# A chained attention and two-MoE kernel: the second MoE's weights converted two thirds of the program earlier, by way of DRAM

## The chip, the cores and the metric

The kernel runs on one core of one Trainium2 chip. The metric is the device time of one execution, in microseconds (us); the median of three runs is 1712.07 us, the runs lie between 1711.86 and 1712.95. Engines are named as the profile names them: PE is TensorE's matmul, PEld its weight load, DVE is VectorE, ACT is ScalarE, POOL is GpSimd, SP is SyncE, which issues all of this kernel's DMAs.

## The reference, cut to what matters

A linear attention, an MoE (a two-layer perceptron with s * relu(h)^2 + b between the layers) and a second MoE (with h * sigmoid(1.702 h)), one behind the other, all in float32:

```python
kv = einsum('bhsd,bhse->bhde', k, v)                 # 8 batches, 8 heads, 576 x 64
o  = einsum('bhsd,bhde->bhse', q, kv)
x  = o / sqrt(mean(o * o) + 1e-6) * g_norm           # -> 4608 tokens x 512
x  = (s * relu(x @ w_in)**2 + b) @ w_out             # 512 -> 2048 -> 512
h  = x @ w2_in
x  = (h * sigmoid(1.702 * h)) @ w2_out
```

The weights reach the device as 64-bit words, two 32-bit halves for each value, and are turned into float32 there.

## The kernel before

**Tiles and steps.** The 4608 tokens are cut into NB = 9 blocks of 512. A block of an MoE has NF = 16 steps, one for each 128 of the 2048 inner features. So there are 2 x 9 x 16 = 288 steps, numbered i = 0 to 287: steps 0 to 143 are the first MoE (block j has steps 16j to 16j + 15), steps 144 to 287 the second. Every matmul operand is split into a high and a low part (hi and lo), and three products are summed: h takes 12 matmuls of 128x512 (`mlp_h`, L255), o takes 12 (`mlp_o`, L295). In the first MoE o's second matmul is the first that reads gl.

**The order within a step** is written out by hand at the end of the kernel and kept as it stands (`manual_schedule`): `mlp_h` of this step on PE; side work of slot 2i; `mlp_act` of this step (relu L263 and square L264 on ACT; in the second MoE sigmoid on ACT, product on DVE); `mlp_o` of the step before on PE; `mlp_g` of this step (gh on ACT, L275 or L278; r, L276, and gl, L279, on DVE); at a block's first step the results of the block before are copied out (`mlp_store`: two by ACT, L304, two by DVE, L302, then four DMAs on SP, L306 or L308); side work of slot 2i + 1. So PE runs h(i), o(i-1), h(i+1), o(i), and ACT and DVE have from the end of h(i) to the second matmul of o(i) for relu to gl. Each engine works through its queue in the order of the program: on ACT, what stands in slot 2i comes before the step's relu.

**Side work** is a list of (slot, order of entry, function). Entries with the same slot keep the order in which they were entered: attention before the second MoE's inputs, these before its weights. There are four kinds.

- The k and v products (`kv_load`, `kv_product`), up to slot 49. Their inputs lie in two buffers of the pool `kp` with the tag "kv", of 5 KB a partition each.
- Attention of block j, during block j - 1, for each head pair p = 0 to 3: `att_product` (PE; ACT's square and sh, L190; DVE's sl, L191) at slot 32(j-1) + 7 + 6p, `att_mean` (PE's two matmuls, then three operations on ACT, L201 to L203) two slots later, `att_newton` (three operations on DVE, L208 to L210) two later, `att_split` (xh on ACT, L219, and the subtraction xl on POOL, L222) two later, which is the slot of the next pair's `att_product`. These slots are odd: each is the second half of a step. `q_load` stands five slots before `att_product`.
- The second MoE's inputs: `x2_load` (SP, from the DRAM tile x2d) and `x2_split` (ACT, L239, and POOL, L240), four for each block.
- The weights. A unit is one of 16 pieces of w_in or w_out (`which` 0 or 1, `f` 0 to 15): 512 KB raw, 128 x 1024 words. `weight(load, slot, gap, conv_at, ...)` enters `w_load` (one DMA on SP, L82 or L87) at `load`, and at slot + gap * conv_at the four parts `w_low` (two operations on ACT, L94 and L95), `w_words` (four on DVE, L101 to L104), `w_hi` (one on ACT, L111) and `w_lo` (one on DVE, L116).

**The second MoE's weights before.** Their 32 units go into the buffers of the first MoE's weights (pool `wp`, one buffer for each unit), so each raw unit waits until the first MoE has used that piece for the last time, in its last block (j = 8, steps 128 to 143). Unit n has slot 259 + 1.75 n with the parts at +0, +1, +2.5 and +4.5, and its load three slots earlier: slots 256 to 318, steps 128 to 159.

The program below prints the functions that the diff touches and what calls them.

Of the kernel before, what the change touches and what calls it, by code (L numbers as in the profile page):

```python
# [7 lines left out]
F32 = mybir.dt.float32  # L8
F32R = mybir.dt.float32r
U32 = mybir.dt.uint32  # L10
# [3 lines left out]
P = 128  # L14
# [4 lines left out]
NF = DFF // P  # L19
NB = B * S // T  # L20
# [4 lines left out]


START = [(-61, -60, -54, -52, -45), (-59, -54, -53, -47, -42), (-54, -48, -48, -43, -41), (-50, -49, -46, -40, -36)]
CONV = [(0, 1, 2, 3), (-0.5, 0, 1, 1.5), (0, 1, 2.5, 4.5)]


@with_exitstack
def kernel(ctx: ExitStack, tc: tile.TileContext, qT, kv_h, kvt, cst,
# [6 lines left out]
    nc = tc.nc  # L39
# [3 lines left out]
    wp = ctx.enter_context(tc.tile_pool(name="wp", bufs=1))  # L43
# [4 lines left out]
    kp = ctx.enter_context(tc.tile_pool(name="kp", bufs=2))  # L48
    dp = ctx.enter_context(tc.tile_pool(name="dp", bufs=1, space=bass.MemoryType.DRAM))
# [26 lines left out]
    conv, W = {}, {}  # L76

    def w_load(m, f, which):
        raw = wp.tile([P, 512, 2], U32, tag=f"w{which}_{f}", name="raw")
        src = w_raw[m][which]  # L80
        if which == 0:
            nc.sync.dma_start(  # L82
                out=raw.rearrange("p (k c) t -> p k (c t)", k=NP),
                in_=src.rearrange("(k p) c -> p k c", p=P)[:, :, f * 2 * P:(f + 1) * 2 * P],
            )
        else:
            nc.sync.dma_start(out=raw.rearrange("p c t -> p (c t)"), in_=src[f * P:(f + 1) * P, :])  # L87
        conv[m, f, which] = raw
# [17 lines left out]

    def w_hi(m, f, which):
        a = conv[m, f, which]
        w = wp.tile([P, 2, 512], F32R, tag=f"w{which}_{f}", name=f"w{which}_{f}")
        W[m, f, which] = (w[:, 0, :], w[:, 1, :])  # L110
        act.activation(w[:, 0, :], a.bitcast(F32), AF.Copy)  # L111

    def w_lo(m, f, which):
        a = conv.pop((m, f, which))
        hi, lo = W[m, f, which]
        dve.tensor_sub(out=lo, in0=a.bitcast(F32), in1=hi.bitcast(F32))  # L116


    kvin, kvs, qin, xT, done = {}, {}, {}, {}, set()
# [196 lines left out]
    def at(slot, fn, *a):  # L316
        side.append((slot, len(side), fn, a))

    def weight(load, slot, gap, conv_at, *unit):
        at(load, w_load, *unit)  # L320
        for n, (i, fn) in enumerate(zip(conv_at, (w_low, w_words, w_hi, w_lo))):
            at(slot + gap * i, fn, *unit)
# [7 lines left out]
    def attention(slots, j, p, o_at, ms_at):  # L330
        at(slots[0], att_product, j, p, o_at)
        at(slots[1], att_mean, j, p, ms_at)
        at(slots[2], att_newton, j, p)
        at(slots[3], att_split, j, p)
# [4 lines left out]
    for p in range(NP):  # L339
        kv_work(-99 + p, START[p][0], 0, p, (pa, pb)[p % 2])  # L340
        at(-99 + p, q_load, 0, p)
        attention(START[p][1:], 0, p, (ps_o, f"o{p}"), (ps_h, "h"))
    weight(-128, -58.5, 3.5, CONV[0], 0, 0, 0)
    weight(-89, -48.5, 4, CONV[0], 0, 1, 0)


    units = [(f - w, w) for f in range(1, NF + 1) for w in range(2) if f - w < NF][1:]
    for n, (f, w) in enumerate(units):
        weight(n - 5, n - 1, 1, CONV[1], 0, f, w)

# [5 lines left out]
    for j in range(1, NB):  # L356
        for p in range(NP):
            slot = 2 * NF * (j - 1) + 7 + 6 * p
# [6 lines left out]
    for j in range(NB):  # L365
        for p in range(NP):
            slot = 2 * NF * (NB + j - 1) + 1 + 3.5 * p
            at(slot, x2_load, j, p)
            at(slot + 3, x2_split, j, p)
    for n in range(2 * NF):  # L370
        slot = 2 * NF * (NB - 1) + 3 + 1.75 * n
        weight(slot - 3, slot, 1, CONV[2], 1, n // 2, n % 2)

    side.sort(key=lambda e: e[:2])
    side.reverse()
# [60 lines left out]
```

## Time and profile before

| | before |
|---|---|
| median of three runs | 1712.07 us |
| the profiled execution's own time | 1712.43 us |
| its span, first to last instruction | 1710.6 us |
| mean granted clock of TensorE | 0.996 |
| PE busy | 1685.7 us (99%) |
| PEld busy | 1380.0 us (81%) |
| ACT busy | 745.7 us (44%) |
| DVE busy | 721.9 us (42%) |
| POOL busy | 96.1 us (6%) |
| DMA: read from, written to HBM | 72.22 MB, 19.79 MB |

A busy share is a mean over stages that differ, and matmuls are pipelined, so that a PE which is shown as busy can still run slower than it might. A step's length is read from the timeline instead: from the first matmul of an h or o to that of the next one. Step numbers are had by counting the h groups of twelve (the trace does not name steps). In a timeline a row is: start in us from the span's beginning, length in us, engine, line, operation, tiles written and read, shape, count, and in brackets the engine's idle time before it and what ended that. In a table by windows a row is: stretch, its length, then the busy time of PE, PEld, DVE, ACT and POOL with the count of instructions, the granted clock, the DMA engines' busy share and GB/s.

### The profile page before, as it was taken

Reading aid. Unit: us, or ns where it says so; the run is one execution under the profiler, and the core shown is the slowest. Engines: PE = TensorE matmul, PEld = TensorE weight load, DVE = VectorE, ACT = ScalarE, POOL = GpSimd, SP = SyncE. Lnnn points to the kernel's source line nnn. Section 1 sums busy time; section 2 is a strip of 40 time slices with the busy share of each in tenths; the row PEclk is TensorE's granted clock in tenths of the full one; section 3 lists DMA queues with packets and bytes.
Section 4 is the critical chain, followed back from the end, with each engine's and each line's share of the span. In section 5 each row is a group of like instructions: output and inputs, shape, how many; then the busy total and the mean of one; then the engine's idle time right before and its main releaser. Section 6 shows DMA issues by size and latency. Waiting matters only on the chain.

```text
span 1710.6 us, 18774 instructions
## 1 busy us (share of the span) xinstructions
PE 1685.7 (99%) x7460; PEld 1380.0 (81%) x7460; DVE 721.9 (42%) x1110; ACT 745.7 (44%) x1218; POOL 96.1 (6%) x82
## 2 busy tenths in 40 slices
PE   7999999999999999999999999999999999999998
PEld 5877888888888888888877788888888888888887
DVE  5997233433434343434578842222222222222222
ACT  5776455545455454555676532222222222222222
POOL 1000000000000000000000000000000000101000
PEclk8999999999999999999999999999999999999999
DMA  7863401010100001010434110101010101000000
GB/s 239 272 210 104 121 19 46 7 47 7 40 13 32 22 1 53 1 44 7 160 124 164 46 50 1 49 0 48 2 44 7 44 7 38 12 27 24 20 7 25
DMA packets 67655, 93.22 MB, mean 54 GB/s; under 512 B 13808, under 2 KB 40432, under 8 KB 67568
## 3 DMA queue, kind: packets, MB, share of 16 engines
q1 hardware_dynamic: 67568, 92.04, 17.0%
q8 instruction: 58, 0.95, 0.2%
q14 instruction: 29, 0.24, 0.0%
HBM read 72.22 MB, written 19.79 MB: 54 GB/s over the span
## 4 chain that ended last, share of the span: by engine, by line
PE 89%; DVE 7%; DMA 1%; ACT 1%; issue 1%; SPq 0%; DVEq 0%; ACTq 0%
PE o L295 42%; PE h L255 42%; PE o_ps L182 2%; DVE cu L103 1%; PE kv L149 1%; DVE w L116 1%; PE ms L198 1%; DVE ca L104 1%; DVE cu L102 1%; DVE gl L279 1%; DVE cu L101 1%; PE kv L150 1%; DVE r L276 0%; DMA kv_in<-in_kv 0%; DVE r L267 0%
## 5 line engine op out<-in xcount | busy, mean ns | idle before, releaser
L255 PE MATMUL h<-xh,w 128*128 128x512 f32 x2304 | 769.0, 395 | 0.1
L255 PEld LDWEIGHTS h<-xh,w 128*128 128x128 f32 x2304 | 433.2, 188 | 95.0 <-issue 1.7
L255 PE MATMUL h<-xl,w 128*128 128x512 f32 x1152 | 449.0, 390 | 0.0
L295 PE MATMUL o<-gh,w 128*128 128x512 f32 x1152 | 378.2, 389 | 0.0
L295 PE MATMUL o<-w,gh 128*128 128x512 f32 x1152 | 356.2, 390 | 3.4 <-ACT gh L278 3.3
L279 DVE TENSOR_TENSOR gl<-r,gh 128x512 fp32r<-128x512 f32 x288 | 228.9, 795 | 113.6 <-ACT gh L278 100.6
L267 DVE TENSOR_TENSOR r<-h,r 128x512 f32<-128x512 f32 x144 | 99.5, 691 | 414.8 <-ACT r L266 414.8
L266 ACT ACTIVATE r<-h 128x512 f32<-128x512 f32 x144 | 85.8, 596 | 414.8 <-PE h L255 414.7
L295 PEld LDWEIGHTS o<-w,gh 128*128 128x128 f32 x1152 | 216.7, 188 | 49.7 <-ACT gh L278 5.0
L255 PEld LDWEIGHTS h<-xl,w 128*128 128x128 f32 x1152 | 216.8, 188 | 47.7 <-issue 2.7
L295 PEld LDWEIGHTS o<-gh,w 128*128 128x128 f32 x1152 | 216.2, 188 | 45.2 <-ACT gh L275 0.4
L276 DVE TENSOR_SCALAR r<-r,cst_sb 128x512 f32<-128x512 f32 x144 | 78.7, 547 | 379.3 <-ACT gh L275 379.1
L295 PE MATMUL o<-gl,w 128*128 128x512 f32 x576 | 224.9, 390 | 3.7 <-DVE gl L279 3.7
L295 PE MATMUL o<-w,gl 128*128 128x512 f32 x576 | 225.0, 391 | 0.0
L263 ACT ACTIVATE r<-h 128x512 f32<-128x512 f32 x144 | 85.7, 595 | 249.3 <-PE h L255 249.3
L278 ACT ACTIVATE gh<-r 128x512 fp32r<-128x512 f32 x144 | 91.1, 633 | 124.7 <-DVE r L267 124.7
L295 PEld LDWEIGHTS o<-gl,w 128*128 128x128 f32 x576 | 108.1, 188 | 28.8 <-DVE gl L279 6.5
L295 PEld LDWEIGHTS o<-w,gl 128*128 128x128 f32 x576 | 108.3, 188 | 24.1 <-DVE gl L279 1.7
L275 ACT ACTIVATE gh<-r,cst_sb 128x512 fp32r<-128x512 f32 x144 | 117.5, 816 | 4.8
L264 ACT ACTIVATE r<-r 128x512 f32<-128x512 f32 x144 | 91.0, 632 | 4.6
L222 POOL TENSOR_TENSOR xl<-y,xh 128x512 fp32r<-128x512 f32 x36 | 47.6, 1323 | 773.7 <-ACT xh L219 414.0
L240 POOL TENSOR_TENSOR xl<-x,xh 128x512 fp32r<-128x512 f32 x36 | 46.8, 1301 | 698.3 <-ACT xh L239 568.4
(53 smaller groups left out, 846.1 us busy)
## 6 DMA issues: line engine op xcount, KB each, us to landing
raw<-in_w_in SPq DMA_DIRECT2D x32, 512.0 KB, 5.7
kv_in<-in_kv SPq DMA_DIRECT2D x32, 512.0 KB, 4.6
raw<-in_w_out SPq DMA_DIRECT2D x32, 512.0 KB, 6.3
x2d<-st SPq DMA_DIRECT2D x36, 256.0 KB, 2.1
x<-x2d SPq DMA_DIRECT2D x36, 256.0 KB, 2.9
out<-st SPq DMA_DIRECT2D x36, 256.0 KB, 2.1
kv_in<-in_kvt SPq DMA_DIRECT2D x32, 64.0 KB, 4.3
qq<-in_qT SPq DMA_DIRECT2D x8, 256.0 KB, 5.1
```

Of the source, the lines that this page charges most:

```text
L222: pool.tensor_sub(out=xl[:, p, :], in0=x, in1=xh[:, p, :].bitcast(F32))
L240: pool.tensor_sub(out=xl[:, p, :], in0=t, in1=xh[:, p, :].bitcast(F32))
L255: pe.matmul(h, lhsT=a[:, cc], rhs=x[:, c, :], start=(n == 0), stop=(n == 3 * NP - 1))
L263: act.activation(r, h, AF.Relu)
L264: act.activation(r, r, AF.Square)
L266: act.activation(r, h, AF.Sigmoid, scale=1.702)
L267: dve.tensor_mul(out=r, in0=h, in1=r)
L275: act.activation(gh, r, AF.Identity, scale=s_col, bias=b_col)
L276: dve.tensor_scalar(out=r, in0=r, scalar1=s_col, scalar2=b_col, op0=ALU.mult, op1=ALU.add)
L278: act.activation(gh, r, AF.Copy)
L279: dve.tensor_sub(out=gl, in0=r, in1=gh.bitcast(F32))
L295: pe.matmul(o, lhsT=a, rhs=x, start=(f == 0 and n == 0), stop=(f == NF - 1 and n == 2))
```

## The change

The 32 units of the second MoE are loaded and converted during the first MoE, in the two "kv" buffers that the k and v products no longer need. Raw words go into one ("raw2"), hi and lo into the other ("w2"). Unit n has slot 60 + 6n (60 to 246), the parts at +0, +1, +2.5 and +4, and its load two slots earlier: a unit every three steps, steps 30 to 125. At +5.5 a new function `w2_store` writes hi and lo (512 KB) to a DRAM tile. During the first MoE's last block a new function `w2_load` reads them into the buffers of the first MoE's weights, each piece after that block has used it: slot 258 + n + n % 2, steps 129 to 145. All new DMAs are on SP. 16.8 MB more are written to DRAM and 16.8 MB more are read.

```diff
-CONV = [(0, 1, 2, 3), (-0.5, 0, 1, 1.5), (0, 1, 2.5, 4.5)]
+CONV = [(0, 1, 2, 3), (-0.5, 0, 1, 1.5), (0, 1, 2.5, 4)]
...
     def w_load(m, f, which):
-        raw = wp.tile([P, 512, 2], U32, tag=f"w{which}_{f}", name="raw")
+        if m == 0:
+            raw = wp.tile([P, 512, 2], U32, tag=f"w{which}_{f}", name="raw")
+        else:
+            raw = kp.tile([P, 512, 2], U32, tag="kv", name="raw2")
...
     def w_hi(m, f, which):
         a = conv[m, f, which]
-        w = wp.tile([P, 2, 512], F32R, tag=f"w{which}_{f}", name=f"w{which}_{f}")
+        if m == 0:
+            w = wp.tile([P, 2, 512], F32R, tag=f"w{which}_{f}", name=f"w{which}_{f}")
+        else:
+            w = kp.tile([P, 2, 512], F32R, tag="kv", name="w2")
+            w2[f, which] = w
...
+    w2, w2d = {}, [[dp.tile([P, 2, 512], F32, name=f"w2d{which}_{f}") for which in range(2)] for f in range(NF)]
+
+    def w2_store(f, which):
+        nc.sync.dma_start(out=w2d[f][which], in_=w2.pop((f, which)).bitcast(F32))
+        del W[1, f, which]
+
+    def w2_load(f, which):
+        w = wp.tile([P, 2, 512], F32R, tag=f"w{which}_{f}", name=f"w{which}_{f}")
+        nc.sync.dma_start(out=w.bitcast(F32), in_=w2d[f][which])
+        W[1, f, which] = (w[:, 0, :], w[:, 1, :])
...
     for n in range(2 * NF):
-        slot = 2 * NF * (NB - 1) + 3 + 1.75 * n
-        weight(slot - 3, slot, 1, CONV[2], 1, n // 2, n % 2)
+        slot = 60 + 6 * n
+        weight(slot - 2, slot, 1, CONV[2], 1, n // 2, n % 2)
+        at(slot + 5.5, w2_store, n // 2, n % 2)
+        at(2 * NF * (NB - 1) + 2 + n + n % 2, w2_load, n // 2, n % 2)
```

## Rows read from the trace of the kernel before

**Rows 1.** Windows: a plain block, the conversion stretch, and its longest gap.
```profile
461.00:548.00 87.00, 87.00 (x386) 71.81 (x385) 33.78 (x46) 45.45 (x70) 5.12 (x4) 1.00 0.06 18
...
896.00:991.00 95.00, 90.73 (x386) 72.29 (x385) 78.34 (x129) 55.60 (x96) 5.66 (x4) 0.98 0.27 94
944.00:951.00 7.00, 4.24 (x13) 3.04 (x12) 6.10 (x12) 3.21 (x6) 0.00 (x0) 0.76 0.29 105
```

**Rows 2.** Timeline of PE: the first matmuls of steps 128 and 160.
```profile
822.16 0.39 PE L255 MATMUL h<-xh,w 128*128 128x512 f32 x1
...
1007.04 0.39 PE L255 MATMUL h<-xh,w 128*128 128x512 f32 x1
```

**Rows 3.** Timelines of PE, DVE and ACT, steps 141 and 142.
```profile
898.42 0.39 PE L295 MATMUL o<-gh,w 128*128 128x512 f32 x1
...
903.86 0.40 PE L295 MATMUL o<-gh,w 128*128 128x512 f32 x1
905.15 0.50 PE L295 MATMUL o<-gl,w 128*128 128x512 f32 x1 [0.89 <-DVE gl L279]
...
898.65 0.42 DVE L101 TENSOR_SCALAR cu<-cu 128x512 f32<-128x512 f32 x1
...
904.40 0.69 DVE L279 TENSOR_TENSOR gl<-r,gh 128x512 fp32r<-128x512 f32 x1
...
901.01 0.63 ACT L111 ACTIVATE w<-ca 128x512 fp32r<-128x512 f32 x1 [3.15 <-DVE ca L104]
901.55 0.58 ACT L263 ACTIVATE r<-h 128x512 f32<-128x512 f32 x1
...
903.55 0.65 ACT L94 ACTIVATE ca<-raw 128x512 uint32<-128x512 uint32 x1
...
904.66 0.62 ACT L111 ACTIVATE w<-ca 128x512 fp32r<-128x512 f32 x1
```

**Rows 4.** Timelines of ACT, DVE, POOL and PE, an attention cycle (steps 69, 70).
```profile
481.97 0.63 ACT L203 ACTIVATE y<-y 128x512 f32<-128x512 f32 x1
483.30 0.60 ACT L263 ACTIVATE r<-h 128x512 f32<-128x512 f32 x1 [0.70 <-PE h L255]
...
488.74 0.60 ACT L263 ACTIVATE r<-h 128x512 f32<-128x512 f32 x1 [3.33 <-PE h L255]
...
495.10 0.60 ACT L263 ACTIVATE r<-h 128x512 f32<-128x512 f32 x1 [1.45 <-PE h L255]
...
486.10 0.69 DVE L279 TENSOR_TENSOR gl<-r,gh 128x512 fp32r<-128x512 f32 x1
...
488.16 0.75 DVE L210 SCALAR_TENSOR_TENSOR y<-o_ps,g_col,y 128x512 f32<-128x512 f32 x1
...
491.54 1.79 DVE L279 TENSOR_TENSOR gl<-r,gh 128x512 fp32r<-128x512 f32 x1
493.75 0.69 DVE L191 TENSOR_TENSOR sl<-sq,sh 128x512 fp32r<-128x512 f32 x1 [0.41 <-ACT sh L190]
...
491.51 1.28 POOL L222 TENSOR_TENSOR xl<-y,xh 128x512 fp32r<-128x512 f32 x1 [38.21 <-issue]
...
495.12 0.39 PE L295 MATMUL o<-gl,w 128*128 128x512 f32 x1
```

**Rows 5.** Timelines of DVE and SP, the first step of a block (step 64).
```profile
457.53 0.69 DVE L279 TENSOR_TENSOR gl<-r,gh 128x512 fp32r<-128x512 f32 x1
...
459.48 0.69 DVE L302 COPY st<-o 128x512 f32<-128x512 f32 x1 [0.65 <-DMA x2d<-st]
...
457.36 3.16 SPq L306 DMA_DIRECT2D x2d<-st  x4
```

**Rows 6.** The tile raw, 820 to 900 us: its loads, 512 KB each.
```profile
DMA to landing us min/median/max: 3.5/4.3/5.4
```

**Rows 7.** Timeline of PE, the longest gap after the start (step 149).
```profile
947.38 1.22 PE L295 MATMUL o<-w,gh 128*128 128x512 f32 x2 [2.77 <-ACT gh L278]
```

**Rows 8.** The chain that ended last, around that gap: start, length, what.
```profile
947.38 4.34 PE o L295 x12
```

## The prediction

> **What bounds the kernel now.** The page's shares put TensorE (PE) first; the table by stage says where it is not the limit. In a block of the first MoE without conversions PE is busy for all of 87.00 us at full clock, VectorE (DVE) for 33.78, ScalarE (ACT) for 45.45; in the stretch where the second MoE's weights are converted, PE is busy for 90.73 of 95.00 us and DVE for 78.34 [rows 1]. The timeline of PE gives the loss. Steps 128 to 159 carry no attention, only the conversions; they run from 822.16 to 1007.04, 184.88 us [rows 2]. A step with nothing beside it takes 5.44 us (first matmuls of o at 898.42 and 903.86 [rows 3]); 32 of them are 174.08. So the conversions cost **10.8 us** where they stand.
>
> The chain of waits, and the timelines behind it, show how a conversion costs PE time [rows 3]. The words start on DVE at 898.65; w_hi, which waits for their last operation, starts on ACT at 901.01, 2.36 us later; the step's relu stands behind w_hi in ACT's queue and starts 0.54 after it, at 901.55. An undisturbed relu starts together with the second matmul of the o that runs then (495.10 and 495.12 [rows 4]), here 0.23 after 898.42. So it was 2.9 us late; gl followed at 904.40, and o's second matmul, due 0.23 after 903.86, ran at 905.15, 1.06 late. A relu may thus be 2.92 - 1.06 = 1.86 us late for nothing; what is beyond, PE loses. That is the gauge for the new place.
>
> **What the change removes.** All 32 conversions leave steps 128 to 159. ACT and DVE keep there what they do in every block, and the 10.8 us go.
>
> **What it adds in steps 30 to 126.** One unit every three steps: two operations on ACT (w_low), four on DVE (words), one each for hi and lo. Busy time is no problem: DVE has 53 us free in a block and ACT 41 [rows 1]. The place in the queues decides. The words of unit n stand behind gl in step 30+3n, and whatever the attention put on DVE in that half step stands before them; w_hi stands before the relu of the next step. The attention also runs in cycles of three steps, but a block has 16, so their phase shifts by block. By the slots the 32 units fall into four classes.
>
> (a) 18 units, with the words alone (n = 1 and 17), in the step of an att_mean (the eight of blocks 2 and 5) or in that of an att_product (the eight of blocks 3 and 6). Alone: gl ends 486.10 + 0.69 - 483.30 = 3.49 after its relu, w_hi starts at 5.85, the next relu at 6.39 instead of 5.44: 0.95 late, free. With att_mean there are two more matmuls in between: free too. With att_product the words stand behind sl, which ends at 493.75 + 0.69 = 494.44; w_hi at 496.80, relu at 497.34 instead of 495.10: 2.24 late, against 1.86 and the next step's two matmuls of the mean (0.45): just free. These 18 cost 0; if the last eight are misjudged by 0.5 us, they cost 4.
>
> (b) 8 units, with the words in the step of an att_newton: n = 0, 13 to 16, 29 to 31. Take the cycle of [rows 4]. The mean's last operation on ACT ends at 482.60; w_low comes next and takes 1.11 (903.55 to 904.66 [rows 3]); relu 483.71 instead of 483.30. gl starts 2.80 after a relu (488.74 to 491.54): 486.51. The newton operations ended 2.81 after gl's start (486.10 to 488.91): 489.32. Then the words; w_hi 2.36 later, 491.68; relu 0.54 later, **492.22 instead of 488.74**, 3.48 late. This next step is also the one of att_split: GpSimd's (POOL) subtraction starts at 491.51, 0.03 before gl, and gl takes 1.79 instead of 0.69. It ended at 493.33, and o's second matmul ran at 495.12: slack 1.79. Lost: 3.48 - 1.79 + 0.06 (905.09 to 905.15) = 1.75 us. In six of the eight an att_product adds 0.92 us of PE time (relu to relu 6.36 against 5.44) which is in that slack; behind the fourth head pair (n = 0 and 16) there is none, and 2.67 are lost. 6 x 1.75 + 2 x 2.67 = **15.8 us**.
>
> On that subtraction: the row has gl ending 0.54 after POOL. The Trainium skill (SBUF — State Buffer, "Who interferes with whom") says that whichever of the two holds the shared port first holds it for its whole instruction and the other fully blocks; by that gl would need its 0.69 after POOL's end, 0.15 more in each of eight places, and the sum would be 1.2 higher. The row is taken.
>
> (c) Two units in the first step of a block (n = 6 and 22), where DVE first copies two results: gl starts at 457.53, the second copy ends at 460.17 [rows 5], 5.44 after the relu. w_hi at 7.80, relu at 8.34 instead of 5.44: 2.90 late, 1.04 lost: 2.1. Two with an att_split and no product (n = 11 and 27): gl ends 4.59 after relu (493.33 - 488.74), next relu 7.49: 2.05 late, 0.2 lost: 0.4.
>
> (d) Two units (n = 12 and 28) whose load stands on SP's queue behind a block's four stores and two query loads. The stores end at 457.36 + 3.16 = 460.52 [rows 5], the queries about 1 us later (an estimate from 0.79 a store), all 2.05 later because of n = 11 and 27: 463.6. A load lands 3.5 to 5.4 us after its issue [rows 6]; taken 3.5, since it is alone. w_low at 467.1, relu at 468.2; due at 457.53 - 2.80 + 2 x 5.44 = 465.6: 2.6 late, 0.7 lost each, **1.5** (5.2 at 5.4 us).
>
> At nothing: the other loads (issued when the words of the unit before are done, over two steps ahead of w_low); the stores of 512 KB (w_hi of the next unit, which needs their buffer, comes over 8 us after lo; a store of this size is not in the trace, the loads' 3.5 to 5.4 are its nearest rows); SP's wait for lo, behind which only transfers stand that are due later; the loads back, 1 MB a step, each needed 15 steps after its issue. The four inputs of block 9 stand between these on SP; if they come late, ACT waits in front of four relus, at most the longest landing less the slack, 5.4 - 1.86 = 3.5 each, 14 in all. Taken as 0, since each is issued two steps or more ahead (the other end belongs to the last rival).
>
> **Sum.** 15.8 + 2.1 + 0.4 + 1.5 = 19.8 added, 10.8 removed: +9.0. The profiled execution took 1712.43 us (its span of 1710.6 and 1.8 around it), 0.36 over the median of the runs; 1712.43 + 9.0 is 1721.4, and on the median of 1712.07 **1721.1**. With the bounds (att_product 0 to 4, loads 0 to 3.7 more, and 0.5 us either way on each of the 12 of (b) and (c)) it spans about 1715 to 1727.
>
> **Rivals.**
>
> *The cover holds* (faster): the late relus have more room than the one row that gauges it shows, some 3.5 us, or w_hi gets through earlier. For it: DVE is more than half idle in these blocks. Against it: 1.06 us were lost at 2.9 late. Then only the gain stays: 1701.3. It decides from a slack 1.75 us larger than the one worked out in (b).
>
> *GpSimd loses the race*: with w_hi directly before it the relu is 0.02 shorter, and the order of POOL and gl hangs on 0.03 us. If gl comes first it takes its 0.69, and (b) falls by 8 x 1.1 = 8.8: 1712.3, no change. Against it: both start from the same gh, at the same distances. The skill's section just named has the same rule, that the order of issue decides who blocks.
>
> *The clock falls*: PE's longest gap, 2.77 us, ended at 947.38 [rows 7]; the granted clock was at its lower level, 1.2 of 2.4 GHz, for part of that stretch (0.76 on the mean of 944 to 951 [rows 1]), and the 12 matmuls behind the gap took 4.34 instead of 2.72 [rows 8], 1.6 more. Against it: the two new gaps would be shorter than that one. The two gaps of 2.67 would add 3.2: 1724.3; all eight, 13: 1734. The Trainium skill (TensorE: Matmul & The Clock Gate, "HAM oscillation — how this bites in real kernels") describes a kernel that falls back at every wait between groups of matmuls; by that it would be the eight.
>
> *The traffic*: 33.6 MB more; if transfers slow each other, units of (a) join (d) at 0.7 to 2.6 each, or the inputs come late: 1725 and over.
>
> **How the numbers follow.** Forecast 0.54 (own range 1715 to 1727), the cover holds 0.17, POOL's order 0.09, clock 0.13, traffic 0.07. A measurement of this kernel tells 0.2% (3.4 us) from no change. Faster: 0.17, the cover. Same: 0.09. Slower: 0.74. The range leaves out the covered case and the far end of clock and traffic: 1711 to 1728.
>
> **What would show it.** In the trace after: no PE gap between step 128 and 160, these 32 steps in 174 us; ACT's w_hi waiting for DVE's ca (L104) some 3 us and more in steps 31, 70, 73, 76, 79, 118, 121 and 124, and PE waiting for their gl by 1.7 to 2.7. I am wrong if PE runs these steps without a gap, if gl is not stretched behind att_split, or if PE waits for loads back or for inputs in step 144 and after.

## The result, and the profile of the changed kernel

The changed kernel takes 1726.63 us (median of four runs, 1724.44 to 1727.41); the kernel before takes 1711.96 in the same comparison. The ratio is 1.0083, 95% interval 1.0066 to 1.0100: slower by 14.7 us. The forecast was slower, by 9.0, and its range of 1711 to 1728 holds the result, near its upper end. The profiled execution took 1726.74 us with a span of 1725.0, against 1710.6.

Lines have moved: h is L274, o L314, relu L282, gh L294, r L295, gl L298, w_low L97 and L98, the words L104 to L107, w_hi L118, w_lo L123, att_split L238 and L241, att_newton L227 to L229. A step's excess is its length, first matmul of h to the next first matmul of h, less that of the same step before (in steps 128 to 159 less 5.44). The sums over the span:

| steps | excess before | excess after |
|---|---|---|
| start, to the end of step 29 | 0 | +1.9 |
| 30 to 127 (the new place) | 0 | +23.2 |
| 128 to 159 (the old place) | +10.8 | 0.0 |
| 160 to the end | 0 | 0.0 |

23.2 + 1.9 - 10.8 = 14.3, the difference of the spans but for 0.1. The row of the start is no part of the change: in other executions of the changed kernel it is 1.0 and 0.1 (last experiment). The gain came in full: step 128 starts at 847.28 and step 160 at 1021.36, 174.08 us. The table by windows of the changed kernel shows both sides (columns as in [rows 1]: stretch, its length, then PE, PEld, DVE, ACT and POOL busy, granted clock, DMA share, GB/s).

```profile
475.00:562.00 87.00, 80.11 (x346) 64.01 (x345) 45.65 (x69) 48.86 (x80) 5.09 (x4) 1.00 0.18 61
856.00:1031.00 175.00, 175.00 (x774) 144.91 (x773) 48.50 (x69) 59.48 (x93) 10.31 (x8) 1.00 0.35 123
```

In the old place PE no longer stops, although the DMA engines move 123 GB/s there, the loads back among it. In the stretch of steps 67 to 80, where a plain block had PE busy for 87.00 of 87.00 us, PE is busy for 80.11. DVE (45.65) and ACT (48.86) are far from full: their load is not what stops PE.

The waits, in us in total, times, longest, of PE and ACT in the new place (250 to 850 us):

```profile
PE o L314 <- DVE gl L298: 10.9, 10, 1.4
PE h L274 <- ACT xh L238: 2.4, 2, 1.2
PE h L274 <- POOL xl L241: 1.7, 2, 0.8
PE o L314 <- ACT gh L294: 1.3, 1, 1.3
...
ACT w L118 <- DVE ca L107: 104.1, 31, 5.8
ACT r L282 <- PE h L274: 73.1, 43, 3.3
...
ACT ca L97 <- DMA raw<-in_w_in: 12.9, 2, 7.1
```

ACT's largest wait in total is w_hi's, for the words: 31 times, 104.1 us. What stands behind it is relu. Here is the very attention cycle of [rows 4], one of the six (timelines of DVE, ACT, POOL and PE, steps 69 to 71; the words and w_hi are unit 13's):

```profile
493.62 0.69 DVE L298 TENSOR_TENSOR gl<-r,gh 128x512 fp32r<-128x512 f32 x1
...
495.67 0.75 DVE L229 SCALAR_TENSOR_TENSOR y<-o_ps,g_col,y 128x512 f32<-128x512 f32 x1
496.34 0.42 DVE L104 TENSOR_SCALAR cu<-cu 128x512 f32<-128x512 f32 x1
...
502.02 1.79 DVE L298 TENSOR_TENSOR gl<-r,gh 128x512 fp32r<-128x512 f32 x1
...
498.70 0.63 ACT L118 ACTIVATE w<-ca 128x512 fp32r<-128x512 f32 x1 [5.77 <-DVE ca L107]
499.24 0.58 ACT L282 ACTIVATE r<-h 128x512 f32<-128x512 f32 x1
...
501.99 1.28 POOL L241 TENSOR_TENSOR xl<-y,xh 128x512 fp32r<-128x512 f32 x1 [43.27 <-DVE r L295]
...
502.13 0.39 PE L314 MATMUL o<-gh,w 128*128 128x512 f32 x1
503.87 0.50 PE L314 MATMUL o<-gl,w 128*128 128x512 f32 x1 [1.35 <-DVE gl L298]
```

Read it from gl (493.62) downwards: att_newton holds DVE until the words start at 496.34; w_hi starts 2.36 later, at 498.70, relu 0.54 after it; gl starts at 502.02, 0.03 behind POOL's subtraction, and takes 1.79; o's second matmul, due 0.23 after 502.13, runs at 503.87: 1.51 late. The matmuls behind the gap lose 0.13 more, and the step's excess is 1.65.

This is where the excess of steps 30 to 127 lies, by the classes of the prediction. The o of a step runs within the next step, so the excess of a late gl stands one step later than the step that the prediction names:

| class | predicted | measured, us (step) |
|---|---|---|
| 18 units, words alone, with att_mean or att_product | 0 | 0 |
| six with att_newton, a product behind | 10.5 | 9.7: 1.65, 1.61, 1.59 (71, 74, 77), 1.65, 1.59, 1.59 (119, 122, 125) |
| two with att_newton of the fourth head pair | 5.3 | 5.2: 2.59 (32), 2.62 (80) |
| two at a block's first step | 2.1 | 1.9: 0.95 (50), 0.94 (98) |
| two at a block's end | 0.4 | 0.6: 0.30 (65), 0.30 (113) |
| two late loads | 1.5 | 5.9: 1.50 (67), 4.37 (115) |

The sum is 23.2 where 19.8 was forecast. The 4.37 of step 115 holds about 1.6 for a fall of the clock: behind the gap the granted clock is at its lower level, 1.2 GHz, for a while, and the matmuls there take longer. Without it the gaps are 21.6 and the two late loads 4.2. The late loads and this fall make the difference, the other classes cost 0.9 less than forecast.

### The profile page after: what moved, and what is told of

The parts are those of the page before. It is cut to its first block, busy times and chain, and to the rows that moved or that the text cites. A ratio compares the mean times of both kernels' runs of the same rounds, so it can differ in the third digit from the quotient of the medians.

```text
span 1725.0 us, 18934 instructions
## 1 busy us (share of the span) xinstructions
PE 1690.4 (98%) x7460; PEld 1381.8 (80%) x7460; DVE 717.6 (42%) x1110; ACT 742.2 (43%) x1218; POOL 95.6 (6%) x82
## 4 chain that ended last, share of the span: by engine, by line
PE 62%; DVE 2%; ACT 2%; DMA 1%; issue 0%; SPq 0%; DVEq 0%
PE o L314 31%; PE h L274 30%; DVE gl L298 1%; PE o_ps L201 0%; ACT gh L294 0%; ACT r L283 0%; DMA raw<-in_w_in 0%; PE ms L217 0%; ACT r L282 0%; DVE r L295 0%; DMA x2d<-st 0%; DVE cu L106 0%; DVE ca L107 0%; ACT w L118 0%; ACT cu L98 0%
## 5 line engine op out<-in xcount | busy, mean ns | idle before, releaser
L274 PE MATMUL h<-xh,w 128*128 128x512 f32 x2304 | 769.6, 395 | 2.6 <-ACT xh L238 2.4
L274 PEld LDWEIGHTS h<-xh,w 128*128 128x128 f32 x2304 | 433.4, 188 | 98.6 <-ACT xh L238 3.3
L274 PE MATMUL h<-xl,w 128*128 128x512 f32 x1152 | 449.3, 390 | 1.7 <-POOL xl L241 1.7
L314 PE MATMUL o<-gh,w 128*128 128x512 f32 x1152 | 380.1, 391 | 1.4 <-ACT gh L294 1.3
L314 PE MATMUL o<-w,gh 128*128 128x512 f32 x1152 | 354.6, 389 | 0.0
L298 DVE TENSOR_TENSOR gl<-r,gh 128x512 fp32r<-128x512 f32 x288 | 231.3, 803 | 113.2 <-ACT gh L297 99.8
L274 PEld LDWEIGHTS h<-xl,w 128*128 128x128 f32 x1152 | 216.7, 188 | 49.7 <-issue 2.7
L314 PEld LDWEIGHTS o<-gh,w 128*128 128x128 f32 x1152 | 217.0, 188 | 47.8 <-ACT gh L294 2.2
L314 PEld LDWEIGHTS o<-w,gh 128*128 128x128 f32 x1152 | 216.3, 188 | 44.9
L314 PE MATMUL o<-gl,w 128*128 128x512 f32 x576 | 226.4, 393 | 12.0 <-DVE gl L298 12.0
L295 DVE TENSOR_SCALAR r<-r,cst_sb 128x512 f32<-128x512 f32 x144 | 78.7, 547 | 358.9 <-ACT gh L294 358.5
L314 PE MATMUL o<-w,gl 128*128 128x512 f32 x576 | 224.1, 389 | 0.0
L282 ACT ACTIVATE r<-h 128x512 f32<-128x512 f32 x144 | 84.9, 590 | 150.1 <-PE h L274 150.1
L314 PEld LDWEIGHTS o<-gl,w 128*128 128x128 f32 x576 | 108.5, 188 | 39.8 <-DVE gl L298 17.8
L314 PEld LDWEIGHTS o<-w,gl 128*128 128x128 f32 x576 | 108.0, 187 | 22.5
L294 ACT ACTIVATE gh<-r,cst_sb 128x512 fp32r<-128x512 f32 x144 | 117.4, 816 | 4.8
L118 ACT ACTIVATE w<-ca 128x512 fp32r<-128x512 f32 x64 | 40.2, 628 | 132.5 <-DVE ca L107 128.7
L241 POOL TENSOR_TENSOR xl<-y,xh 128x512 fp32r<-128x512 f32 x36 | 47.5, 1322 | 798.8 <-ACT xh L238 314.0
```

The costliest lines, as they stand in the source:

```text
L241: pool.tensor_sub(out=xl[:, p, :], in0=x, in1=xh[:, p, :].bitcast(F32))
L274: pe.matmul(h, lhsT=a[:, cc], rhs=x[:, c, :], start=(n == 0), stop=(n == 3 * NP - 1))
L282: act.activation(r, h, AF.Relu)
L294: act.activation(gh, r, AF.Identity, scale=s_col, bias=b_col)
L295: dve.tensor_scalar(out=r, in0=r, scalar1=s_col, scalar2=b_col, op0=ALU.mult, op1=ALU.add)
L298: dve.tensor_sub(out=gl, in0=r, in1=gh.bitcast(F32))
```

## The experiments

Each is compared with the kernel before on the same chip (its medians there: 1712.50 in the first four experiments, 1713.03 in the next three). Tables of excess are read from the timelines as above.

### w_hi half a step later

```diff
-CONV = [(0, 1, 2, 3), (-0.5, 0, 1, 1.5), (0, 1, 2.5, 4)]
+CONV = [(0, 1, 2, 3), (-0.5, 0, 1, 1.5), (0, 1, 3, 4)]
```

> The changed kernel with w_hi half a step later (at +3 instead of +2.5), so that on ScalarE it stands behind gh of its step and no longer in front of relu; nothing else. Theory: what costs time is the late w_hi at the head of ScalarE's queue. Then the gaps of the attention steps (14.9 us in eight places) and of the two block starts and two block ends (2.5 us) go, and those behind the late loads (5.9 us with the clock's fall) shrink to 0 to 3, since the block's stores come 1.9 us earlier: 1701.5 to 1706. Rival: VectorE's load itself delays r and gl; it does the same work in the same order here, so the time stays at 1724 to 1727.

Measured: 1702.74 us (1702.03 to 1703.32), ratio to the kernel before 0.9944, interval 0.9929 to 0.9960. The waits of ACT and PE in this kernel, 250 to 850 us:

```profile
ACT w L118 <- DVE ca L107: 0.3, 2, 0.2
...
PE o L314 <- DVE gl L298: 0.2, 1, 0.2
```

The one wait of 104.1 us is gone, and with it 22.7 of the 23.2 us; 0.51 is left in step 115, behind a late load. DVE does the same operations in the same order, so its load is not the cause: the rival falls. The late loads shrank with the rest, as the block ends no longer delayed the stores in front of them. Timelines of SP, first the changed kernel (step 65 starts at 462.67), then this one (at 457.11):

```profile
464.69 3.16 SPq L325 DMA_DIRECT2D x2d<-st  x4
...
457.21 3.17 SPq L325 DMA_DIRECT2D x2d<-st  x4
```

The stores start 2.02 after the step's first matmul in the one and 0.10 in the other.

The loads of units 12 and 28 still come late here, and so test the slack of 1.86 twice more (timelines of ACT and PE):

```profile
467.31 0.58 ACT L282 ACTIVATE r<-h 128x512 f32<-128x512 f32 x1
...
745.69 0.58 ACT L282 ACTIVATE r<-h 128x512 f32<-128x512 f32 x1
...
749.22 0.50 PE L314 MATMUL o<-gl,w 128*128 128x512 f32 x1 [0.22 <-DVE gl L298]
```

The first relu was due at 465.47 (5.44 after the one before): 1.84 late, and step 67 has no excess. The second was due at 743.37, 2.32 late; o's second matmul was due at 748.84 and is 0.38 late, so the slack was 1.94.

### The loads two slots earlier

```diff
-        weight(slot - 2, slot, 1, CONV[2], 1, n // 2, n % 2)
+        weight(slot - 4, slot, 1, CONV[2], 1, n // 2, n % 2)
```

> The changed kernel with each raw load two slots earlier (four before its unit's slot), so that the loads of units 12 and 28 stand in front of a block's four stores on SyncE's queue; nothing else. Theory: only the gaps in steps 67 and 115 go, 1.5 and 2.7 to 4.4 us: 1720.5 to 1723. Rival: those gaps come from the words and w_hi of the units before, not from the loads: 1726 to 1727.

Measured: 1721.02 us (1719.86 to 1722.08), ratio 1.0050 (1.0036 to 1.0064). Steps 67 and 115 have no excess at all; all others have what they had, but step 32 has 4.20 instead of 2.59 (a fall of the clock, below). PE's waits, 250 to 850 us:

```profile
PE o L314 <- DVE gl L298: 9.1, 8, 1.4
```

Eight waits for gl are left of ten, and none for gh. So the loads' place behind the block's stores on SP is what made those two gaps, and nothing else depends on it.

### Both

The two edits together.

> The changed kernel with w_hi half a step later and the loads two slots earlier together. Theory: no gap is left between steps 30 and 160; the time of the kernel before less its 10.8 us of conversion gaps: 1701 to 1703. Rival: one of the two moves only shifts the wait (w_hi later leaves lo, the store and the next load late): 1705 to 1712.

Measured: 1702.02 us (1701.60 to 1703.15), ratio 0.9940 (0.9928 to 0.9953). The table by windows of this kernel, all of the new and the old place in one row:

```profile
260.00:980.00 720.00, 720.00 (x3168) 592.89 (x3167) 353.42 (x529) 402.30 (x631) 44.62 (x33) 1.00 0.28 93
```

PE is busy for 720.00 of 720.00 us; no step from 30 to 287 has an excess. **This version is faster than both kernels.** Its time does not tell it from the first experiment (the intervals overlap); its trace does, by the 0.51 us of step 115.

### The words ahead of att_newton

```diff
-        at(slots[2], att_newton, j, p)
+        at(slots[2] + 0.25 * (j > 0), att_newton, j, p)
```

> The changed kernel with att_newton a quarter slot later, so that where it shares a half step with a unit's words the words come first on VectorE; nothing else is moved. Theory: in the eight attention steps the words end 2.2 us earlier, w_hi and relu too, relu is some 1.3 us late instead of 3.5: the six gaps of 1.6 us go, the two of 2.6 fall to 0.5 or less; the block starts, block ends and late loads stay: 1711 to 1713.5. Rival: the sum of VectorE's work counts, not its order: 1724 to 1727.

Measured: 1712.81 us (1710.74 to 1714.21), ratio 1.0001 (0.9992 to 1.0010). Timelines of DVE, ACT and PE in the cycle of above:

```profile
490.45 0.69 DVE L298 TENSOR_TENSOR gl<-r,gh 128x512 fp32r<-128x512 f32 x1
491.06 0.42 DVE L104 TENSOR_SCALAR cu<-cu 128x512 f32<-128x512 f32 x1
...
494.76 0.75 DVE L229 SCALAR_TENSOR_TENSOR y<-o_ps,g_col,y 128x512 f32<-128x512 f32 x1
...
493.43 0.63 ACT L118 ACTIVATE w<-ca 128x512 fp32r<-128x512 f32 x1 [3.67 <-DVE ca L107]
493.96 0.58 ACT L282 ACTIVATE r<-h 128x512 f32<-128x512 f32 x1
...
495.10 0.39 PE L314 MATMUL o<-gh,w 128*128 128x512 f32 x1
495.61 1.10 PE L201 MATMUL o_ps<-qq,kvbd 128*128 128x320 f32 x4
```

With the same work in another order, w_hi starts 2.98 after gl (490.45 to 493.43) instead of 5.08 (493.62 to 498.70), and the gaps of 1.6 are gone. The two of 2.6 fell to 0.54 each. In place of the six there is a new wait of 0.35 that was not foreseen: att_newton now ends at 495.51, and att_product, which writes into the PSUM buffer that it reads, starts at 495.61 instead of directly behind the matmul at 495.10. The order on DVE decides, not the amount.

### att_split's subtraction on VectorE

```diff
-        pool.tensor_sub(out=xl[:, p, :], in0=x, in1=xh[:, p, :].bitcast(F32))
+        (dve if j else pool).tensor_sub(out=xl[:, p, :], in0=x, in1=xh[:, p, :].bitcast(F32))
```

> The changed kernel with att_split's subtraction on VectorE instead of GpSimd (blocks 1 to 8), behind gl; nothing else. Theory: gl is no longer stretched from 0.7 to 1.8 us there. The six attention gaps of 1.6 fall to about 0.5 (6.6 less), the block ends' 0.6 go and with them up to 4 of the late loads'; the two gaps of 2.6 behind the fourth head pair stay, since there PE waits for that subtraction itself: 1715 to 1720. Rival: the stretch of gl costs nothing beside a late relu: 1724 to 1727.

Measured: 1717.80 us (1715.78 to 1719.71), ratio 1.0028 (1.0019 to 1.0038). Timelines of DVE (the same cycle) and of PE (step 32):

```profile
500.83 0.69 DVE L298 TENSOR_TENSOR gl<-r,gh 128x512 fp32r<-128x512 f32 x1
501.44 0.68 DVE L241 TENSOR_TENSOR xl<-y,xh 128x512 fp32r<-128x512 f32 x1
...
268.37 0.49 PE L274 MATMUL h<-xh,w 128*128 128x512 f32 x1 [1.21 <-ACT xh L238]
269.83 0.50 PE L274 MATMUL h<-xl,w 128*128 128x512 f32 x1 [0.96 <-DVE xl L241]
```

Without POOL beside it gl takes 0.69, and the six gaps are 0.55 each: 1.06 of each came from POOL's subtraction beside gl. The block ends' gaps (65, 113) are gone. The late loads' are 3.5 in all, which is little less than the 4.2 of the changed kernel without the fall of the clock, and its repeats below have 4.0 and 3.8: the part of the expectation that gave them up to 4 is not shown. Step 50's grew from 0.95 to 1.47. Of the time gained, 1.8 us lie before step 30, in block 0's own attention (steps 7, 10 and 13 are 1.1 shorter each than in the kernel before); they have nothing to do with the new place. The two behind the fourth head pair stay, as expected: there PE waits for the subtraction's own result, now DVE's. They measure 4.33 each in this profile, since the clock fell after both.

### Without the way through DRAM

The two DMAs of `w2_store` and `w2_load` are left out; the second MoE uses W of the first.

> The changed kernel without the stores to DRAM and the loads back (64 transfers of 512 KB); conversions at the new place as they are, and the second MoE computes with the first one's weights, so that part of the result is left out. Theory: the way through DRAM costs nothing: 1724 to 1727.5, with the same gaps in the same steps. Rival: the traffic slows the loads: the gaps in steps 67 and 115 shrink and the time falls by 2 to 6, to 1720 to 1724.5.

Measured: 1724.55 us (1723.74 to 1725.49), ratio 1.0068 (1.0053 to 1.0083). PE's waits, 250 to 850 us (here o is L311 and gl L295):

```profile
PE o L311 <- DVE gl L295: 10.9, 10, 1.4
```

The same row as with the traffic. Steps 30 to 127 have 23.4 us of excess, against 23.2, each with one fall of the clock in it; steps 67 and 115 have 2.25 and 2.05, and step 80 4.21 with the fall. So 33.6 MB of transfers cost PE nothing that the trace shows. The intervals of the two ratios overlap, so the times alone would not decide it.

### The kernel before, with w_hi half a slot later

```diff
-CONV = [(0, 1, 2, 3), (-0.5, 0, 1, 1.5), (0, 1, 2.5, 4.5)]
+CONV = [(0, 1, 2, 3), (-0.5, 0, 1, 1.5), (0, 1, 3, 4.5)]
```

> The kernel before with w_hi half a slot later (at +3 instead of +2.5), conversions at their old place. Theory: of its 10.8 us the gaps that follow a late w_hi (steps 142 and 156, and part of 147 to 149) shrink, those of late loads and of VectorE's full queue stay: 1706 to 1711. Rival: there VectorE is simply full and a later w_hi only moves the wait: 1711 to 1713.

Measured: 1708.99 us (1708.06 to 1709.72), ratio 0.9977 (0.9968 to 0.9987). In steps 128 to 159 6.7 of 10.8 us are left. ACT's waits of this kernel, 820 to 1010 us:

```profile
ACT gh L278 <- DVE r L267: 36.6, 17, 5.5
...
ACT w L111 <- DVE ca L104: 1.8, 2, 1.3
```

In the kernel before w_hi waits for 21.8 us in all, here for 1.8; but gh waits for r for 36.6 us instead of 27.7, and up to 5.5 us at a time instead of 3.6. Of the 4.1 that went in the trace, 1.6 is no effect of the order: the longest gap, in step 149, is there as before, and the kernel before had a fall of the clock behind it in its profile (excess 4.39) where this one has none (2.77). With a unit every 0.9 steps DVE's queue now holds the chain, and this move on ACT gives back no more; other orders at the old place were not tried. With the same cure the new place takes 1702.74, so it is worth something of its own.

### The changed kernel again, twice

No edit.

> The changed kernel, unaltered, in another execution. Theory: the gaps of steps 30 to 127 are the same within 0.1 us in the same steps (21.6 without falls of the clock), and what is above the kernel before + 10.8 comes from short falls of the granted clock, of about 1.65 each, whose number and place differ from one execution to the next; the 1.7 lost before the first h is such a fall and no part of the change. Rival: the loss at the start returns at the same place, 10 us from the span's beginning, and so belongs to the change.

> The same once more. Theory: the same gaps, another set of clock falls; time 1722.8 + 1.65 for each fall other than the long one of the start, within 1. Rival: the same set of falls as in the first profile.

Measured: 1728.94 us and 1724.67 us (one execution each). The gaps stand in the same steps; without falls of the clock they differ by 0.1 or less, except at the two late loads, where they lie between 1.5 and 2.7 and the expectation of 0.1 missed. Windows of the first and of the second execution (the third number from the end is the mean granted clock; 1.00 is 2.4 GHz throughout, 0.79 is part of the stretch at 1.2):

```profile
270.00:278.00 8.00, 5.95 (x19) 4.52 (x19) 4.71 (x6) 4.81 (x9) 1.26 (x1) 0.79 0.11 41
559.00:567.00 8.00, 5.95 (x18) 4.21 (x17) 4.18 (x6) 4.69 (x8) 1.27 (x1) 0.79 0.12 47
```

```profile
270.00:278.00 8.00, 6.80 (x29) 5.42 (x30) 5.21 (x7) 4.51 (x9) 1.26 (x1) 1.00 0.16 60
559.00:567.00 8.00, 7.42 (x25) 5.94 (x26) 4.21 (x6) 4.23 (x7) 0.52 (x1) 0.79 0.31 113
```

The first execution fell to the lower level after the gaps of steps 32 and 80 and once more at 115 (excess 4.12, 4.22, 3.70), the second after step 80 alone (4.23, beside 2.61 at 32). The formula, 1722.8 + 1.65 for each fall, gives 1727.8 and 1724.5; the first is off by 1.2, a little more than was said; 1.0 of that was lost before step 30. The loss of 1.7 us before the first h did not come back at its place in either.

## Why the prediction was right, point by point

**What is removed.** The step held to the hundredth: 174.08 us for steps 128 to 159. One thing the prediction did not say of its 10.8: 1.6 of them were the fall of the clock in step 149, which it counts as certain here and as a rival at the new place. No load back and no input came so late that PE waited; the first input of block 9 made ACT wait 1.4, within its slack. The loads back land in 4.0 us in the median and the stores in 2.9, from the page of the changed kernel:

```profile
w2d<-w SPq DMA_DIRECT2D x32, 512.0 KB, 2.9
w<-w2d SPq DMA_DIRECT2D x32, 512.0 KB, 4.0
```

**The mechanism.** Queue position, not load: shown by the first experiment (w_hi behind gh and nothing else: 1702.74 instead of 1726.63) and from the other side by the fourth (words ahead of att_newton). The gauge of 1.86 us of slack, taken from one place in the old trace, carried over: the two late loads of the first experiment test it (1.84 late for nothing, 1.94 of slack), the four units of class (c) come within about 0.1 each, and the 18 that were called free are free, the att_product ones too, whose margin was worked out at 0.07.

**The six attention gaps.** 1.75 was forecast, 1.59 to 1.65 came, and the match is a little closer than the sum deserves. What it forecast is how late o's second matmul is, and that is 1.51: relu is 3.27 late instead of 3.48, since the sum lets w_low and the words start when the operation before them ends, and the trace starts them 0.08 to 0.09 earlier (the words at 496.34, where 495.67 + 0.75 is 496.42). The 0.13 that the matmuls behind the gap lose was not in the sum and makes up for half of that. That POOL still starts first is in the timeline (501.99 against 502.02), and its share of 1.1 was confirmed at 1.06 by moving it away. The rule of the Trainium skill weighed there (SBUF — State Buffer, "Who interferes with whom") would have gl end its full 0.69 after POOL; in the row after, gl ends at 503.81, 0.54 after POOL's 503.27. The row was right to take.

**The two behind the fourth head pair.** The size was right (2.67 forecast, 2.59 and 2.62 measured), the wait named was not. The prediction has PE waiting for gl in o. In the timeline of PE at step 32 it stops earlier:

```profile
272.08 0.50 PE L274 MATMUL h<-xh,w 128*128 128x512 f32 x1 [1.21 <-ACT xh L238]
273.43 0.50 PE L274 MATMUL h<-xl,w 128*128 128x512 f32 x1 [0.84 <-POOL xl L241]
273.76 0.39 PE L274 MATMUL h<-xh,w 128*128 128x512 f32 x1
273.99 0.39 PE L314 MATMUL o<-gh,w 128*128 128x512 f32 x1
274.22 0.39 PE L314 MATMUL o<-gl,w 128*128 128x512 f32 x1
```

The fourth pair's att_split makes the last quarter of the next block's input, and that block's first h runs before the o that waits for gl. xh stands behind the late gh on ACT and xl behind xh on POOL; h's last three matmuls wait for both, and when they are through, gl is there (274.22 follows 273.99 at once). Two waits that end together cost the time of one. The prediction missed the reader that comes first; it was lucky that both come from the same late relu.

**The late loads.** The mechanism held (the second experiment takes both gaps away), its size did not: 0.7 each was forecast. The failing term is the landing, "taken 3.5, since it is alone". The timelines of SP, ACT and PE for unit 28:

```profile
756.51 1.93 SPq L85 DMA_DIRECT2D raw<-in_w_in  x1
...
762.91 0.66 ACT L97 ACTIVATE ca<-raw 128x512 uint32<-128x512 uint32 x1 [7.12 <-DMA raw<-in_w_in]
...
766.16 0.49 PE L314 MATMUL o<-gh,w 128*128 128x512 f32 x1 [1.33 <-ACT gh L294]
767.54 0.50 PE L314 MATMUL o<-gl,w 128*128 128x512 f32 x1 [0.88 <-DVE gl L298]
```

The load needs 6.40 us from the start of its issue to w_low (762.91 - 756.51), unit 12's 4.61 (468.89 to 473.50), and the issue alone takes 1.93 in this execution. It is not alone: the block's last stores and the query loads were issued within 1.5 us before it and are still under way (such a store lands 2.0 us or more after its issue here). The store of w2 is not what makes it long: without any, in the run without traffic, unit 12 needs 5.37 and unit 28 5.61. What makes up the length of these landings was not taken apart. The bound that the prediction gave with it (5.2 in all) holds the 4.2 without the clock, though the landing of unit 28 is outside its 3.5 to 5.4. Then the clock fell in the gap, and added about 1.6 to step 115. Windows of the changed kernel around that gap and in the start:

```profile
8.00:16.00 8.00, 7.33 (x28) 4.70 (x28) 2.23 (x7) 2.44 (x5) 0.00 (x0) 0.79 1.07 327
766.00:774.00 8.00, 6.95 (x21) 5.01 (x21) 4.63 (x8) 3.76 (x7) 0.00 (x0) 0.79 0.21 66
```

**The clock.** This rival came true in part, beside the forecast. The executions of the changed kernel that were profiled have one, three and one falls of about 1.65 between steps 30 and 128, and the first has another in the start. They fall behind the largest gaps (steps 32, 80, 115) and not behind every one: the same gap of 2.6 at step 32 was followed by none in two of the three. The Trainium skill (TensorE: Matmul & The Clock Gate, "HAM oscillation — how this bites in real kernels") describes a kernel that falls at every wait, with waits longer than the gaps here; of the eight attention gaps none, two and one were followed by a fall in the three executions. The medians fit: gaps alone give 1711.96 - 10.8 + 21.6 = 1722.8, and the four runs lie 1.6 to 4.6 above it, one to three falls. So of the 5.7 us by which the change cost more than forecast, 2.7 are the late loads (1.5 and 2.7 without the fall, instead of 1.5 together), the other classes took 0.9 less than their sum, and 3.9 are left, which the three profiles put down to falls of the clock and to the start. For the runs without a profile that is argued, not shown; their mean granted clock goes the same way, 0.996 in the fastest (1724.44), 0.995 in 1726.52 and in the profiled 1726.74, 0.994 in the slowest (1727.41).

**The other rivals.** The cover did not hold (no place shows more than 0.1 of room beyond the 1.86), POOL did not lose the race (gl takes 1.7 us or more behind all eight att_splits), the traffic costs nothing that can be seen. The stores were put at nothing for 8 us of room before w_hi of the next unit; unit 1's waited 0.2 us for the store of unit 0, and it cost nothing.

## What to carry to other kernels

When work is moved to a place where the engines have time, ask for each moved instruction what stands behind it in its engine's queue and when its own input is ready. An instruction that waits, put in front of the one that the busiest engine needs next, costs what its wait takes beyond the slack; here the same instruction half a step later cost almost nothing. Two cycles of different length (here a unit every three steps, a block of 16) meet in every phase, so the cost is the sum over the bad meetings, and the mean load does not show it: with w_hi moved by half a step the same change is worth 10 us instead of costing 15.

## What was not expected of the hardware

The loads of raw words, all of 512 KB, landed after very different times between 250 and 820 us of the changed kernel (the tile raw, SP's issues):

```profile
DMA to landing us min/median/max: 3.4/3.6/6.4
```

The longest is unit 28's, whose issue alone took 1.93 us on SP where unit 12's took 0.43. A gap of about 2.6 us on PE is followed by a fall of the granted clock in some executions and not in others, at the same place of the same program.
